# Stores of the twenty-product sums moved to GpSimd's queue, and the kept sums weighed one block later

## The chip, the cores and the metric

The kernel runs on one core of a Trainium2 chip. Its time is device microseconds (us) for one execution; several executions were timed, and the figure given is their median. A profile of one execution, taken by the hardware profiler, stands beside it.

The engines of a core run side by side and each works through its own list of instructions in order. TensorE (PE in the profile) multiplies matrices, and its weight loads (PEld) overlap its multiplications. VectorE (DVE) and ScalarE (ACT) do elementwise work and evict accumulators. GpSimd (POOL) does elementwise work too. SyncE (SP) does nothing here but issue transfers. A transfer is issued by an engine's list, so an engine that waits before it issues one transfer issues none of the later ones either.

## The reference, cut to what matters

An attention block gives a matrix x of 4352 rows and 128 columns. Then comes a mixture of eight experts, with all eight weighted by P, which is found from x by eight rounds of normalization:

```python
for e in range(E):                       # E = 8
    h = np.maximum(x @ w1[e], 0.0)       # w1[e]: 128 x 1024
    ye = h @ w2[e]                       # w2[e]: 1024 x 128
    out += P[:, e:e + 1] * ye
```

All of it is in 32-bit floats. P is positive, so the weight can be put on x before the first product instead of on ye after the second.

## The kernel before: the parts concerned

The rows of x are split into groups. The first groups use experts 0 and 1 and run while P is not yet known; their results stay unweighted in SBUF, in tiles called `kept`. Then come five groups of three tiles of 256 columns each (`t == 3` below), for the remaining experts, and a last group of two tiles. A pair of a group and an expert is an item. An item of a three-tile group has two blocks of eight steps.

The second product of such an item is done with twenty smaller products in place of twenty-four, and for it sixteen of the twenty need sums and differences of blocks of w2. In the first three-tile group GpSimd computes these sums for each expert, once, and the result (128 partitions x 2048 floats, 1 MB) is stored to memory. The later groups load them back.

```python
def sums_of_four(e, w2):
    ws = pools[0].tile([P, len(FORMS), FO // 4, H2], F32, tag="ws4", name="ws4")   # two buffers
    if e in stored_four:
        nc.sync.dma_start(out=ws, in_=stored_four[e])            # L230: later groups load
        return ws
    ...
    for ns, x, y, off in FOURS:                                  # ten instructions, L242
        tc.keep_in_program_order(nc.gpsimd.tensor_tensor(ws[:, c:c + len(ns)], blocks(x), blocks(y), ...))
        c += len(ns)
    stored_four[e] = dram.tile([P, len(FORMS), FO // 4, H2], F32, name=f"ws4{e}")
    nc.sync.dma_start(out=stored_four[e], in_=ws)                # L246: the store
    return ws
```

The weights of expert e are loaded by SyncE, w1 by L190 and w2 by L191. The weighted input of an item, `xe`, is made by a load of P's row spread over the partitions (L674, SyncE) and a product with x on GpSimd (L678). The `kept` tiles are weighed in the same way, from a buffer called `pb`:

```python
def load_w(e, ...):
    w1 = wpool.tile([P, F], F32, tag="w1", name="w1")                        # two buffers of each
    w2 = wpool.tile([P, FO, DM], F32, tag="w2", name="w2")
    nc.sync.dma_start(out=w1, in_=moe_w1[e])                                 # L190
    nc.sync.dma_start(out=w2, in_=moe_w2[e].rearrange(...))                  # L191

def weights_of(e, lo, n, tag):
    pb = pools[0].tile([P, 3 * NT3], F32, tag=tag, name=tag)[:, 0:n]         # two buffers
    tc.keep_in_program_order(nc.sync.dma_start(out=pb, in_=pT[e:e + 1, lo:lo + n].to_broadcast([P, n])))  # L674
    return pb

def weigh(out, x, pb):
    tc.keep_in_program_order(nc.gpsimd.tensor_tensor(out, x, pb, op=Alu.mult))                            # L678

def weigh_kept(g, i):
    lo, n, t, es, _ = groups[g]
    ys = [kept[e][:, lo:lo + n * t] for e in range(es[0])]
    if i < len(ys):
        weigh(ys[i], ys[i], weights_of(i, lo, n * t, "pb"))
        return
    for y in ys[1:]: ...                                                     # L702: the second is added to the first
```

At the first block of an item (q == 0) the next item is prepared:

```python
if q == 0:
    for i in (j, j + 1, ...):
        ... prepare_x(i)        # xe: L674, L678
        ... prepare_w(i)        # w1, w2, and sums_of_four
...
if q == 0:
    if weighted and 1 <= es.index(e) <= es[0] + 1:
        weigh_kept(g, es.index(e) - 1)
```

TensorE's part is two functions. The first product of a step is L914 (`a<-xe,w`), evicted by ScalarE (L918). The twenty products are L1099 (`s<-hx,ws`, `s<-hb,ws`, and with `w` where no sum is needed); they follow the first products of their block by eight steps, that is by one block.

Of the kernel before, what the change touches and what calls it, by code (L numbers as in the profile page):

```python
# [50 lines left out]
def kernel(  # L51
# [12 lines left out]
    nc = tc.nc  # L64
# [147 lines left out]
    stored, stored_four = {}, {}  # L212
# [13 lines left out]
    def sums_of_four(e, w2):  # L226

        ws = pools[0].tile([P, len(FORMS), FO // 4, H2], F32, tag="ws4", name="ws4")
        if e in stored_four:
            nc.sync.dma_start(out=ws, in_=stored_four[e])  # L230
            return ws

        def blocks(bs):
            b = w2[:, bs[0][1]::4, H2 * bs[0][0]:H2 * (bs[0][0] + 1)].unsqueeze(1)
            if len(bs) == 1:
                return b
            step = (bs[1][1] - bs[0][1]) * DM + (bs[1][0] - bs[0][0]) * H2
            return AP(tensor=b.tensor, offset=b.offset, ap=[b.ap[0], [step, 2], *b.ap[2:]])

        c = 0  # L240
        for ns, x, y, off in FOURS:
            tc.keep_in_program_order(nc.gpsimd.tensor_tensor(ws[:, c:c + len(ns)], blocks(x), blocks(y),  # L242
                                                             op=Alu.subtract if off else Alu.add))
            c += len(ns)
        stored_four[e] = dram.tile([P, len(FORMS), FO // 4, H2], F32, name=f"ws4{e}")
        nc.sync.dma_start(out=stored_four[e], in_=ws)  # L246
        return ws


# [399 lines left out]
    def direct_of(j):  # L649
        return items[j][0] in DIRECT  # L650
# [4 lines left out]
    def prepare_w(j):  # L655
        g, e = items[j]
        three = groups[g][2] == 3
        if j == 0:
            loaded_w[j] = first_w
        elif items[j - 1][1] == e or not groups[g][4]:  # L660
            before = [i for i in range(j) if items[i][1] == e and i in loaded_w]
            loaded_w[j] = loaded_w[before[-1]] if before else load_w(e, False)
            if three and tiles_of(j - 1) == 2:
                loaded_w[j] = *loaded_w[j][0:2], sums_of_four(e, loaded_w[j][1])
        else:
            loaded_w[j] = load_w(e, not three, again=groups[g][4])
            if three:
                if g == len(groups) - 2 and e in groups[-1][3]:
                    sums_of_two(e, loaded_w[j][1], True)
                loaded_w[j] = *loaded_w[j][0:2], sums_of_four(e, loaded_w[j][1])  # L670

    def weights_of(e, lo, n, tag):
        pb = pools[0].tile([P, 3 * NT3], F32, tag=tag, name=tag)[:, 0:n]
# [6 lines that stand above are left out]
    def prepare_x(j):  # L680
        g, e = items[j]
        lo, n, t, es, weighted = groups[g]
        x = xT[:, lo:lo + t * n]
        if not weighted:
            sources[j] = x
            return
        xe = weights_of(e, lo, t * n, "xe")
        for sl in (slice(0, 512), slice(512, 768)) if j == first_weighted else (slice(0, t * n),):
            weigh(xe[:, sl], x[:, sl], xe[:, sl])
        sources[j] = xe  # L690
# [3 lines left out]
# [7 lines that stand above are left out]
        for y in ys[1:]:  # L701
            tc.keep_in_program_order(nc.gpsimd.tensor_tensor(ys[0], ys[0], y, op=Alu.add))  # L702
        if t == 2:
            k1, k2 = ys[0][upper, 0:n], ys[0][upper, n:2 * n]
            tc.keep_in_program_order(nc.gpsimd.tensor_tensor(k1, k1, k2, op=Alu.subtract))
# [335 lines left out]
    def last_products():  # L1041

        k = len(blocks) - 2
        one, two_ = ([[(b, p) for p in ps] for ps in seven(b)] for b in (k, k + 1))
        f = last_rooms(len(groups) - 1)[4]
        return one + held[:2] + two_ + held[2:4] + [[(k + 1, (both, f, 2, 0, 0))]] + held[4:]

    def kept_to_sums(g):

        lo, n, *_ = groups[g]  # L1050
        k1, k2 = (kept[0][:, lo + t * n:lo + (t + 1) * n] for t in range(2))
        for i, s, x in ((1, 0, k1), (1, 1, k1), (2, 0, k2), (3, 1, k2)):
            into(g, ident[:, H2 * s:H2 * (s + 1)], x, i, s, 0)
# [52 lines left out]
    def second(k, p):  # L1106
        into(items[blocks[k][0]][0], *p)

    def steps():

        todo, sums_at, t = {}, {}, 0
        for k in range(len(blocks) + 5):
            if k == len(blocks) - 2:
                ctx.enter_context(tc.manual_schedule(engines={engines.DVE, engines.PE, engines.Activation}))
            if k == len(blocks):
                for i, ps in enumerate(last_products()):
                    todo.setdefault(t + i, []).extend(ps)
            if k < len(blocks):
                j, q = blocks[k]
                g, e = items[j]  # L1120
                lo, n, tiles, es, weighted = groups[g]
                if q == 0:
                    for i in (j, j + 1, j + 2 if 0 < j and j + 2 < first_weighted else j):
                        if i < len(items) and i not in sources and (pools or i < first_weighted):
                            prepare_x(i)
                        if i < len(items) and i not in loaded_w and (pools or i < first_weighted):
                            prepare_w(i)
                if j == 0 and q == 2:
                    prepare_w(2)
                if q == 1 and j + 1 < first_weighted and not direct_of(j + 1) and loaded_w[j + 1][2] is None:  # L1130
                    w1, w2, _ = loaded_w[j + 1]
                    w = w1, w2, sums_of_two(items[j + 1][1], w2)
                    loaded_w.update({i: w for i in loaded_w if items[i][1] == items[j + 1][1]})
                if q == 0:
                    if weighted and 1 <= es.index(e) <= es[0] + 1:
                        weigh_kept(g, es.index(e) - 1)
                if k == len(blocks) - HELD:
                    kept_to_sums(g)
                m, step, sums_ = (four if tiles == 3 else two)(k)
                products = twenty if tiles == 3 else eight if g in DIRECT else seven  # L1140
            for c in range(m if k < len(blocks) else 4):
                if k < len(blocks):
                    step(c)
                for do in sums_at.pop(t, ()):
                    do()
                while soon:
                    soon.pop(0)()
                for b, p in todo.pop(t, ()):
                    second(b, p)
                if k < len(blocks) and c == 0:  # L1150
                    for i in range(2, 10):
                        sums_at.setdefault(t + i, []).append(lambda i=i, f=sums_: f(i))
                    if k < len(blocks) - 2:
                        for i, ps in enumerate(products(k)):
                            todo.setdefault(t + LAG + i, []).extend((k, p) for p in ps)
                share = n / 480 * (16 / 15 if g in DIRECT else 1)
                if k >= len(blocks):
                    while later:
                        later.pop(0)()
                elif later and (tiles == 3 or c % 2 or share > 0.9):  # L1160
                    later.pop(0)()
                yield share
                t += 1
        while soon:
            soon.pop(0)()
        while later:
            later.pop(0)()

    work = steps()
    owed = [0.0]

# [97 lines left out]
```

## Time and profile before

| | before |
|---|---|
| time, median of 3 | 920.12 us (920.08 to 920.75) |
| span in the profile | 918.0 us |
| TensorE busy | 911.2 us (99%) |
| VectorE busy | 678.9 us (74%) |
| ScalarE busy | 421.6 us (46%) |
| GpSimd busy | 204.0 us (22%) |
| mean transfer rate | 140 GB/s |
| first three-tile group, seven items | about 184 to 318 us of the span |
| stores concerned (L246) | 7 of 1024 KB, issued from 191.6 to 307.5 us, 4.7 to 5.1 us to landing |

In the views, a line names the source line of the kernel, the engine, the operation, what it writes and from what (`ws<-w`), and how often. In a timeline the first two columns are the start and the length in us, and a bracket at the end says how long the engine sat idle before and what released it. SPq is SyncE's list, which only issues transfers; it is not counted as busy. "xe<-pT" is the load of a row of P.

### The profile page before, as it was taken

How to read it: one execution, taken by the hardware profiler on the slowest of the kernel's cores; microseconds unless marked ns; L12 is line 12 of the kernel's file. 1: busy time of each engine (PE TensorE's matmuls, PEld its weight loads, DVE VectorE, ACT ScalarE, POOL GpSimd, SP SyncE). 2: the span in 40 equal slices, each digit the busy share in tenths (PEclk: the TensorE clock that was granted, in tenths of full speed). 3: DMA queues.
4: the chain of work that ended last, by engine and by line, in shares of the span. 5: the costliest groups of instructions: out<-in, count | busy, mean ns of one | idle time of the engine just before them, and what ended most of it. 6: DMA issues, size and time to landing. Idle time of an engine off the chain costs nothing.

```text
span 918.0 us, 18893 instructions
## 1 busy us (share of the span) xinstructions
PE 911.2 (99%) x7442; PEld 637.4 (69%) x7442; DVE 678.9 (74%) x1173; ACT 421.6 (46%) x915; POOL 204.0 (22%) x212
## 2 busy tenths in 40 slices
PE   9999999999999999999999999999999999999997
PEld 6777544466666677777777777777777655556886
DVE  7678699888776798666975656956567976758665
ACT  3455555554444454444544444544445444445443
POOL 3121100175545421201210010110100243210220
PEclk9999999999999999999999999999999999999999
DMA  9994100213454535534364343454445456453640
GB/s 254 308 273 163 54 1 1 70 64 127 148 150 139 186 119 174 165 110 150 114 185 134 117 143 112 132 187 127 133 122 165 130 170 195 162 166 92 177 153 13
DMA packets 91305, 128.15 MB, mean 140 GB/s; under 512 B 25392, under 2 KB 69504, under 8 KB 86480
## 3 DMA queue, kind: packets, MB, share of 16 engines
q1 hardware_dynamic: 88384, 121.42, 42.7%
q0 software_dynamic: 1600, 5.36, 2.1%
q8 instruction: 58, 0.95, 0.4%
q10 hardware_dynamic: 1232, 0.16, 0.1%
q14 instruction: 31, 0.25, 0.1%
HBM read 107.88 MB, written 19.05 MB: 138 GB/s over the span
## 4 chain that ended last, share of the span: by engine, by line
PE 97%; DVE 2%; ACT 1%; issue 0%; POOL 0%; DVEq 0%; POOLq 0%
PE a L914 51%; PE s L1099 41%; PE a L347 1%; PE a L462 1%; PE a L114 1%; DVE hb L931 1%; PE a L314 0%; PE s L376 0%; PE a L426 0%; PE s L392 0%; DVE cs L602 0%; PE a L496 0%; PE a L392 0%; ACT hb L918 0%; DVE rs L596 0%
## 5 line engine op out<-in xcount | busy, mean ns | idle before, releaser
L914 PE MATMUL a<-xe,w 128*64 128x256 f32 (+1 forms) x2560 | 569.8, 470 | 0.0
L918 ACT ACTIVATE hb<-a 128x256 f32<-128x256 f32 (+4 forms) x408 | 195.0, 480 | 241.5 <-PE a L914 209.3
L914 PEld LDWEIGHTS a<-xe,w 128*64 128x64 f32 x2560 | 263.0, 137 | 50.8 <-issue 1.8
L918 ACT ACTIVATE hx<-a 128x256 f32<-128x256 f32 (+1 forms) x360 | 167.3, 465 | 213.5 <-PE a L914 191.6
L1099 PE MATMUL s<-hb,ws 128*64 128x256 f32 (+3 forms) x1312 | 256.1, 395 | 0.2 <-DVE hb L931 0.2
L1099 PE MATMUL s<-hx,ws 128*64 128x256 f32 x1280 | 233.9, 379 | 0.0
L978 DVE TENSOR_TENSOR hb<-hb 128x512 f32<-128x512 f32 (+1 forms) x204 | 133.5, 664 | 102.8 <-ACT hb L918 98.8
L978 DVE TENSOR_TENSOR hx<-hx 128x512 f32<-128x512 f32 (+1 forms) x204 | 149.8, 744 | 65.0 <-ACT hx L918 60.2
L1099 PEld LDWEIGHTS s<-hb,ws 128*64 128x64 f32 x1312 | 134.9, 137 | 87.8 <-issue 64.5
L678 POOL TENSOR_TENSOR xe<-xT,xe 128x768 f32<-128x768 f32 (+2 forms) x41 | 80.3, 1958 | 481.2 <-DMA xe<-pT 377.0
L1099 PEld LDWEIGHTS s<-hx,ws 128*64 128x64 f32 x1280 | 132.7, 137 | 71.6 <-issue 50.3
L914 PE MATMUL a<-xT,w 128*64 128x416 f32 (+3 forms) x512 | 119.7, 462 | 0.0
L1099 PE MATMUL s<-hb,w 128*64 128x256 f32 (+3 forms) x536 | 114.2, 408 | 0.0
L1099 PE MATMUL s<-hx,w 128*64 128x256 f32 x384 | 76.0, 379 | 0.0
L931 DVE TENSOR_TENSOR hb<-hb 128x416 f32<-128x416 f32 (+7 forms) x84 | 60.7, 723 | 18.0 <-ACT hb L918 14.0
L1099 PEld LDWEIGHTS s<-hb,w 128*64 128x64 f32 x536 | 54.1, 137 | 19.0 <-issue 6.5
L914 PEld LDWEIGHTS a<-xT,w 128*64 128x64 f32 x512 | 48.9, 137 | 25.5 <-issue 15.7
L242 POOL TENSOR_TENSOR ws<-w 128x256 f32<-128x256 f32 (+1 forms) x70 | 60.5, 899 | 8.1 <-DMA w<-in_moe_w_dram 5.2
L931 DVE TENSOR_TENSOR hx<-hx 128x256 f32<-128x256 f32 (+1 forms) x65 | 39.5, 612 | 24.0 <-ACT hx L918 22.8
L1099 PEld LDWEIGHTS s<-hx,w 128*64 128x64 f32 x384 | 40.8, 137 | 6.6
L978 DVE TENSOR_TENSOR pqg<-hb 128x512 f32<-128x512 f32 x68 | 40.5, 637 | 0.0
L978 DVE TENSOR_TENSOR pqg<-hx 128x512 f32<-128x512 f32 x68 | 35.0, 554 | 0.0
(181 smaller groups left out, 485.0 us busy)
## 6 DMA issues: line engine op xcount, KB each, us to landing
w<-in_moe_w_dram SPq DMA_DIRECT2D x82, 512.0 KB, 5.5
ws<-ws SPq DMA_DIRECT2D x34, 1024.0 KB, 5.0
xe<-pT SPq DMA_DIRECT2D x34, 384.0 KB, 4.1
ws<-ws SPq DMA_DIRECT2D x12, 512.0 KB, 3.6
ph<-qa SPq DMA_DIRECT2D x12, 288.0 KB, 4.7
rb<-qb SPq DMA_DIRECT2D x3, 1152.0 KB, 7.2
pb<-pT SPq DMA_DIRECT2D x6, 384.0 KB, 8.3
kx<-in_k_dram SPq DMA_DIRECT2D x4, 544.0 KB, 4.0
```

Of the source, the lines that this page charges most:

```text
L114: nc.tensor.matmul(warm[:, 0:P], ones, ones, start=True, stop=True)
L242: tc.keep_in_program_order(nc.gpsimd.tensor_tensor(ws[:, c:c + len(ns)], blocks(x), blocks(y), op=Alu.subtract if off else Alu.add))
L347: nc.tensor.matmul(pv[64 * s:64 * (s + 1), i], kp[0:n, H * t + h].rearrange("p i j -> p (i j)"), vx[0:n, slots[h], t, :], start=(t == 0 an ...
L462: nc.tensor.matmul(pn[64 * s:64 * (s + 1), t, 2 * i:2 * i + 2].rearrange("p h d -> p (h d)"), ph[:, i, s, 64 * t:64 * (t + 1)], kvs[b % 2] ...
L678: tc.keep_in_program_order(nc.gpsimd.tensor_tensor(out, x, pb, op=Alu.mult))
L914: nc.tensor.matmul(ph[sl], loaded_w[j][0][:, P * f + H2 * s:P * f + H2 * (s + 1)], sources[j][:, lo:hi], start=True, stop=True, tile_posit ...
L918: nc.scalar.activation(out=out, in_=ph, func=Act.Relu)
L931: nc.vector.tensor_tensor(out, a, b, op=Alu.subtract)
L978: nc.vector.tensor_tensor(out if not isinstance(out, tuple) else places(*out), places(*a), places(*b) if isinstance(b, tuple) else b, op=A ...
L1099: nc.tensor.matmul(sums[g][i][H2 * s:H2 * (s + 1), n * place:n * (place + 1)], w, x, start=c == 1, stop=c == per, tile_position=(0, H2 * s))
```

## The change

The store of the sums is issued by GpSimd, in its program order, directly behind the ten instructions that make them, and no longer by SyncE. So SyncE no longer stands in front of the store until GpSimd is done, and what is behind it in SyncE's list, the next item's `xe` and w1, can be issued earlier. The weighing of the kept sums, with its load and GpSimd's product, moves from the first block of an item to the second.

```diff
         stored_four[e] = dram.tile([P, len(FORMS), FO // 4, H2], F32, name=f"ws4{e}")
-        nc.sync.dma_start(out=stored_four[e], in_=ws)
+        tc.keep_in_program_order(nc.gpsimd.dma_start(out=stored_four[e], in_=ws))
         return ws
...
-                if q == 0:
-                    if weighted and 1 <= es.index(e) <= es[0] + 1:
-                        weigh_kept(g, es.index(e) - 1)
+                if q == 1 and weighted and 1 <= es.index(e) <= es[0] + 1:
+                    weigh_kept(g, es.index(e) - 1)
```

The order of instructions on TensorE, VectorE and ScalarE is the same in both kernels. GpSimd's list gains the seven stores and is otherwise in the same order. SyncE's list loses them; apart from that only one load differs in place: the second `pb` of the next group (rows from 512) stands before the `xe`, w1, sums and w2 of an item instead of behind them.

## The prediction

> **What bounds the kernel now.** I read the busy shares by slice and the chain of waits of the page first, then the waits of TensorE alone, then SyncE's own waits, and last the timelines around the seven stores.
>
> ```profile
> PE   9999999999999999999999999999999999999997
> ...
> PE 97%; DVE 2%; ACT 1%; issue 0%; POOL 0%; DVEq 0%; POOLq 0%
> ```
>
> TensorE is at nine tenths or more in every slice but the last, and 97% of the chain that sets the end is TensorE's. GpSimd and SyncE, the only engines whose lists change, have no visible share. Busy matmuls are modelled, so I looked for hidden pauses too. TensorE's waits in the whole span are these three:
>
> ```profile
> PE a L114 <- POOL own L116: 1.0, 1, 1.0
> PE a L392 <- ACT kvz L362: 0.6, 1, 0.6
> PE s L1099 <- DVE hb L931: 0.2, 1, 0.2
> ```
>
> None is near a store. The busy time by stretch says the same: 20.00 of 20.00 us in every stretch from 200 to 400 us. And the pace is even: SyncE's w2 load, which waits for TensorE, goes out at 232.62, 251.57, 270.53 and 289.48 us, an item every 18.95 us; in the next group, where no store is made, at 365.29, 384.25 and 403.20, again 18.95. A stage slowed by the stores would show a longer item than one without them. So at most a fraction of a microsecond can be removed.
>
> Then, what the change aims at, from SyncE's waits (us in total, times, longest):
>
> ```profile
> SPq L674 <- PE a L914: 175.9, 23, 8.6
> ...
> SPq L246 <- POOL ws L242: 111.4, 7, 17.0
> ```
>
> SyncE stands 111.4 us in front of the seven stores until GpSimd has made the sums, with later loads behind it. Its timeline around the last store:
>
> ```profile
> 289.48 0.92 SPq L191 DMA_DIRECT2D w<-in_moe_w_dram  x1
> 307.52 0.33 SPq L246 DMA_DIRECT2D ws<-ws  x1
> 307.93 0.38 SPq L674 DMA_DIRECT2D xe<-pT  x1
> 308.37 0.91 SPq L190 DMA_DIRECT2D w<-in_moe_w_dram  x1
> 309.38 0.96 SPq L230 DMA_DIRECT2D ws<-ws  x1
> 310.40 0.64 SPq L191 DMA_DIRECT2D w<-in_moe_w_dram  x1
> 317.48 0.32 SPq L674 DMA_DIRECT2D xe<-pT  x1
> ```
>
> Five transfers go out within 3 us, 4 MB with the store. The item that uses this `xe` and w1 begins at 317.48 (that is when the next `xe` is released by TensorE). GpSimd's and the weight loads' timelines there:
>
> ```profile
> 299.62 7.87 POOL L242 TENSOR_TENSOR ws<-w 128x256 f32<-128x256 f32 x10 [2.74 <-DMA w<-in_moe_w_dram]
> 314.93 1.82 POOL L678 TENSOR_TENSOR xe<-xT,xe 128x768 f32<-128x768 f32 x1 [7.44 <-DMA xe<-pT]
> ```
>
> ```profile
> 317.07 0.35 PEld L1099 LDWEIGHTS s<-hx,w 128*64 128x64 f32 x2
> 317.60 0.26 PEld L914 LDWEIGHTS a<-xe,w 128*64 128x64 f32 x4 [0.17 <-issue]
> ```
>
> The `xe` is ready at 314.93 + 1.82 = 316.75, 0.7 us early. The w1, issued at 308.37, took 9.1 us to land by the line's own view: 317.47. Its first weight load stands at 317.60, after 0.17 us of idle time; the matmuls behind it start at 317.63, 0.34 us after those before them at 317.29, where 0.21 is the pace. This is the one pause, about 0.13 us, that I can tie to the stores.
>
> **What the Trainium skill says.** "DMA: Bandwidth & Descriptors", section "Issuing engines are not separate DMA queues", says that transfers issued by SyncE, ScalarE and GpSimd run on the same 16 DMA engines, and that a second issuing engine saves only the sequencer's time, which is usually small. Here the traces show why it is not small: the sequencer is not busy but waits, in order, 17.0 us at most. The same page, section "Anatomy of one DMA — SWDGE (gpsimd) path", fits a GpSimd transfer as about 2.0 us plus the bytes at 436 GB/s. For 1,048,576 bytes that gives an estimate of 4.4 us; SyncE's stores took 4.7 to 5.1 us, so no great change is to be expected. "SBUF — State Buffer", section "SBUF: two separate sides", warns that GpSimd cannot write descriptors while certain VectorE instructions hold their shared port. The trace has GpSimd's other transfers: issuing one took 0.54 to 0.64 us on average by line (L433, L437, L486, L488), with VectorE busy beside it. So the warning does not show as a large cost.
>
> **The change part by part.**
> 1. SyncE loses seven issues of 0.33 us and 111.4 us of standing still. Neither is on the chain. What counts is how late its followers come. The needed times: an item starts every 18.95 us, at 241.7, 260.6, 279.6, 298.5 and 317.5; its `xe` and w1 are needed then, its sums one block, 9.5 us, later (the first L1099 weights of the last item are loaded at 308.03, so this fits). Before, `xe` was ready at 240.2, 258.6, 277.5, 296.9 and 316.75: margins of 1.5, 2.0, 2.1, 1.6 and 0.7 us. The last sums were ready at 299.62 + 7.87 = 307.49: a margin of 0.5 us. Everything was just in time.
> 2. Afterwards `xe` and w1 go out when TensorE frees their buffers, at the item's start: for the last one 298.5 instead of 307.9. `xe` lands about 4.1 us later (median of its row), w1 about 5.5 us later (median of its row): 304. w2, issued at 289.48, lands with less beside it: 289.48 + 5.5 = 295.0 instead of 299.6. The ten sums run from 295.0 to 303.8 (8.8 us as in the items before), the store's issue to 304.4, the weighing of `xe` to 306.2. Needed at 317.5: a margin of 11 us instead of 0.7. For the sums 308.0 - 303.8 = 4.2 us instead of 0.5. Gained on the chain: the 0.13 us pause.
> 3. GpSimd gains seven issues of about 0.6 us, 4 us on an engine busy for 9.3 to 11.7 of each 20 us there. Cost on the chain: 0.
> 4. The move by a block: GpSimd's order stays, so the product with `kept` (1.8 to 2.3 us) stands between the same neighbours. On SyncE one `pb` issue (0.57 us) comes ahead of an `xe` that TensorE frees at 355.42. The twelve output stores before it end at 354.2; adding 0.57 gives 354.75, still earlier. And that `xe` was ready at 359.75 + 1.92 = 361.7 for an item that begins at 374.4. Cost: 0. In the last group the lists are the same; its final `kept` is ready at 877.7 and used at 882.4 us.
>
> The sum is -0.13 us, rounded by the spread of the times before (0.67 us) to "no change that matters": 919.97, written as 920.0.
>
> **The rivals.** (a) The stores held TensorE up unseen, and freeing SyncE brings several microseconds. For it: 111.4 us of standing, margins of 0.5 to 2 us. Against it: the same 18.95 us per item with and without stores. It would make some 910 to 917. (b) GpSimd becomes the late one: if a store's issue took as long as a VectorE stretch of work, say 5 us, the sums of the next item would still have 4 us of margin and `xe` 11, so seven such issues cost nothing; only at 10 us each would TensorE wait, some 5 us each, 7 x 5 = 35 us, 955 in all. The 0.6 us issues before speak against it. (c) The store, now free to collide with other loads, delays w2 of the next item. By the times above it runs from 304 to 309 for the last item, while w2 of the item after needs TensorE at 308.5; in the middle items the store ends before w2 is issued (265 to 270, w2 at 270.5). A delay of 1 to 2 us would be taken from a margin of 4. No time. (d) The pause at 317.5 disappears but the two halves of the array run on in another phase: before it the weight loads are 13.2 us per 20, after it 15.6, at the same pace per item. A tenth of a microsecond either way at later changes of shape.
>
> **Range and chances.** The three times before spread by 0.67 us, and the effects named are 0.1 to 0.2 us. So eight in ten lie within about 0.6 us of 920.0: 919.4 to 920.6. Two per cent is 18 us, which neither rival (a) nor anything seen can bring: 0.01 faster. Rival (b) at its worst reaches it: 0.01 slower. Within 2%: 0.98.
>
> **What would show it right or wrong.** Right: SyncE's wait for the sums is gone from its waits, with L674 and L190 issued at item starts; TensorE's pace stays 18.95 us; no 0.17 us idle time at the weight load near 317.5; `xe` and the sums ready 4 to 11 us ahead; GpSimd has seven issues of about 0.6 us. Wrong: new waits of TensorE for GpSimd or for a transfer, items longer than 18.95 us between 200 and 320 us, GpSimd issues of many microseconds, or a time outside the range with a pace that did change, which would mean that "busy" hid a slower TensorE.

## The result and the profile after

| | before | after |
|---|---|---|
| time, median | 920.13 us (919.5 to 920.75) | 923.76 us (922.61 to 924.81, and one of 1063.66) |
| span in the profile | 918.0 us | 921.1 us |
| TensorE busy | 911.2 us | 911.6 us |
| VectorE busy | 678.9 us | 689.0 us |
| GpSimd busy | 204.0 us | 206.5 us |

One of the six executions of after ran at a granted clock of 0.851 and took 1063.66 us; the median of the other five is 923.67 us, and the ratios in this text are of executions at full clock alone. The ratio of after to before is 1.0036, with a 95% interval of 1.0023 to 1.0050. The kernel became slower by 2 to 5 us: less than 2%, but more than its spread, and outside the range that was predicted.

Two of TensorE's waits are new. One, 0.5 us for `kT` (L302), is at 7.5 us of the span, before anything that the change touches: the first load of `kx` landed later in this execution. It comes and goes between the kernels below (0 to 1.3 us) and is no effect of the change. The other is one (us in total, times, longest):

```profile
PE s L1099 <- DVE hx L978: 2.2, 2, 2.0
```

Twenty-product matmuls waited 2.0 us for VectorE, and 0.2 us once more at 205.5 us, not for GpSimd or for a transfer. TensorE's timeline of after at the long wait:

```profile
198.95 0.59 PE L914 MATMUL a<-xe,w 128*64 128x256 f32 x2
201.54 0.65 PE L1099 MATMUL s<-hx,ws 128*64 128x256 f32 x4 [2.00 <-DVE hx L978]
```

What held VectorE stands in its own timeline of after:

```profile
193.17 7.46 DVE L741 TENSOR_TENSOR z<-x,z 128x384 f32<-128x384 f32 x1 [1.77 <-ACT x L750]
200.55 0.94 DVE L978 TENSOR_TENSOR hx<-hx 128x512 f32<-128x512 f32 x1
```

The same addition before:

```profile
192.62 0.56 DVE L741 TENSOR_TENSOR z<-x,z 128x384 f32<-128x384 f32 x1 [1.77 <-ACT x L750]
```

One addition of 384 columns took 7.46 us instead of 0.56. It is counted as busy, so the page shows no wait of VectorE, only 10 us more of busy time, 6.9 of them in this addition. GpSimd's timeline of after says what ran beside it:

```profile
192.43 0.60 POOL L246 DMA_DIRECT2D ws<-ws  x1 [0.30 <-POOL ws L242]
193.05 1.83 POOL L678 TENSOR_TENSOR xe<-xT,xe 128x768 f32<-128x768 f32 x1
194.84 6.10 POOL L242 TENSOR_TENSOR ws<-w 128x256 f32<-128x256 f32 x10
201.23 0.61 POOL L246 DMA_DIRECT2D ws<-ws  x1 [0.30 <-POOL ws L242]
```

The addition lasts from 193.17 to 200.63, that is, from just behind the first store's issue to near the end of eleven GpSimd products without a pause. (GpSimd's spans in a profile are rough; by them the addition ended 0.3 us before the last of the eleven, so some ten of them went ahead of it.) The products were fast for it: ten sums in 6.10 us, against 7.87 to 9.13 us before. In the kernel before, the second item's product came only at 197.6 us, because its `xe` waited behind the store in SyncE's list; the addition at 192.6 had no GpSimd product beside it.

What the change was for did happen. SyncE's wait for the sums is gone from its list of waits, and the last item of the group had its `xe` at 305.97 + 1.82 = 307.8 for a start at 320.8 us: 13 us ahead instead of 0.7.

### The profile page after: what moved, and what is told of

Same layout as the page of the kernel before. It is cut to its first block, busy times and chain, and to the rows that moved or that the text cites. A ratio compares the mean times of both kernels' runs of the same rounds, so it can differ in the third digit from the quotient of the medians.

```text
span 921.1 us, 18899 instructions
## 1 busy us (share of the span) xinstructions
PE 911.6 (99%) x7442; PEld 533.8 (58%) x7442; DVE 689.0 (75%) x1173; ACT 421.7 (46%) x915; POOL 206.5 (22%) x219
## 4 chain that ended last, share of the span: by engine, by line
PE 95%; DVE 3%; ACT 1%; DMA 1%; issue 0%; SPq 0%; DVEq 0%; ACTq 0%
PE a L914 49%; PE s L1099 42%; PE a L347 1%; DVE z L741 1%; PE a L462 1%; DMA kx<-in_k_dram 1%; DVE hb L931 1%; PE a L314 0%; PE s L376 0%; PE a L426 0%; DVE hx L978 0%; PE s L392 0%; DVE cs L602 0%; PE a L496 0%; PE a L392 0%
## 5 line engine op out<-in xcount | busy, mean ns | idle before, releaser
L914 PE MATMUL a<-xe,w 128*64 128x256 f32 (+1 forms) x2560 | 516.2, 470 | 0.0
L914 PEld LDWEIGHTS a<-xe,w 128*64 128x64 f32 x2560 | 200.1, 137 | 86.6 <-issue 1.6
L1099 PE MATMUL s<-hb,ws 128*64 128x256 f32 (+3 forms) x1312 | 228.7, 395 | 0.2 <-DVE hb L931 0.2
L978 DVE TENSOR_TENSOR hb<-hb 128x512 f32<-128x512 f32 (+1 forms) x204 | 132.2, 658 | 102.2 <-ACT hb L918 98.5
L1099 PE MATMUL s<-hx,ws 128*64 128x256 f32 x1280 | 205.4, 379 | 2.2 <-DVE hx L978 2.2
L978 DVE TENSOR_TENSOR hx<-hx 128x512 f32<-128x512 f32 (+1 forms) x204 | 156.3, 777 | 57.5 <-ACT hx L918 52.4
L1099 PEld LDWEIGHTS s<-hb,ws 128*64 128x64 f32 x1312 | 104.9, 137 | 116.7 <-issue 86.6
L1099 PEld LDWEIGHTS s<-hx,ws 128*64 128x64 f32 x1280 | 102.4, 137 | 103.2 <-issue 74.2
L1099 PE MATMUL s<-hb,w 128*64 128x256 f32 (+3 forms) x536 | 106.9, 408 | 0.0
L1099 PE MATMUL s<-hx,w 128*64 128x256 f32 x384 | 67.8, 379 | 0.0
L1099 PEld LDWEIGHTS s<-hb,w 128*64 128x64 f32 x536 | 46.8, 137 | 24.0 <-issue 6.5
L978 DVE TENSOR_TENSOR pqg<-hb 128x512 f32<-128x512 f32 x68 | 41.3, 649 | 0.0
L1099 PEld LDWEIGHTS s<-hx,w 128*64 128x64 f32 x384 | 33.2, 137 | 11.5
L978 DVE TENSOR_TENSOR pqg<-hx 128x512 f32<-128x512 f32 x68 | 36.4, 575 | 0.0
```

Source lines behind the costliest of these rows:

```text
L914: nc.tensor.matmul(ph[sl], loaded_w[j][0][:, P * f + H2 * s:P * f + H2 * (s + 1)], sources[j][:, lo:hi], start=True, stop=True, tile_posit ...
L978: nc.vector.tensor_tensor(out if not isinstance(out, tuple) else places(*out), places(*a), places(*b) if isinstance(b, tuple) else b, op=A ...
L1099: nc.tensor.matmul(sums[g][i][H2 * s:H2 * (s + 1), n * place:n * (place + 1)], w, x, start=c == 1, stop=c == per, tile_position=(0, H2 * s))
```

## The experiments

Three theories stood at first. **A:** GpSimd's products for the second item start 4.6 us earlier, and so collide with a busy stretch of VectorE; any kernel with so early a product stalls. **B:** it is the later weighing of the kept sums that costs the time. **C:** it is the issuing of a transfer by GpSimd that lets VectorE be held. Each kernel was timed against the kernel before on the same chip, in three rounds.

**The store alone.** The weighing of the kept sums stays at the first block:

```diff
-        nc.sync.dma_start(out=stored_four[e], in_=ws)
+        tc.keep_in_program_order(nc.gpsimd.dma_start(out=stored_four[e], in_=ws))
```

> Only the store moves to GpSimd's queue; the kept sums are weighed at the first block as before. Theory A (the stall is one VectorE addition, z<-x,z near 193 us, held off by GpSimd's back-to-back products for 7.5 us because the product for the second item now starts at 193 instead of 197.6 us): the same stall, 2 to 3 us of TensorE's time, 922.5 to 924.5 us. Rival B (the later weighing of the kept sums, which lines up two GpSimd products at 230 us, costs the time): 920.

Measured: 923.03 us, ratio 1.0034 (1.0023 to 1.0046). The addition took 7.75 us, and TensorE waited 2.3 us for hx L978. The store carries the loss; A and C both expect this, B does not.

**The weighing alone.** The stores stay with SyncE; the weighing moves to the second block:

```diff
-                if q == 0:
-                    if weighted and 1 <= es.index(e) <= es[0] + 1:
+                if q == 1 and weighted and 1 <= es.index(e) <= es[0] + 1:
```

> Only the weighing moves by a block; the stores stay with SyncE. Theory A: no stall near 199 us, 919.5 to 920.7 us. Rival B: 922.5 to 924.5.

Measured: 920.57 us, ratio 1.0004 (0.9996 to 1.0013). The addition took 0.56 us. B falls.

**The store by SyncE, but late.** Against after:

```diff
-        tc.keep_in_program_order(nc.gpsimd.dma_start(out=stored_four[e], in_=ws))
+        owed_stores.append((stored_four[e], ws))
...
         xe = weights_of(e, lo, t * n, "xe")
+        pay_stores()          # nc.sync.dma_start for each one owed
```

> The changed kernel, but each store is issued by SyncE, behind the load of the next xe. GpSimd issues no transfer, and its product for the second item can still follow the first sums at once, at about 192 us. Theory A, from the early product: z<-x,z is held off again, for 1.8 us at least and perhaps to the end of the sums (about 200), 920.5 to 924. Rival C (it is GpSimd's writing of the transfer's descriptors that holds VectorE): z<-x,z takes 0.6 us as before and the time is 920.

Measured: 919.97 us, ratio 1.0000 (0.9991 to 1.0008). GpSimd's product came even earlier than in after, and VectorE was not held for long. The timelines of this kernel, VectorE first:

```profile
192.66 1.15 DVE L749 TENSOR_TENSOR z<-x,z 128x384 f32<-128x384 f32 x1 [1.77 <-ACT x L758]
193.73 1.22 DVE L986 TENSOR_TENSOR hx<-hx 128x512 f32<-128x512 f32 x1
```

```profile
191.57 1.82 POOL L685 TENSOR_TENSOR xe<-xT,xe 128x768 f32<-128x768 f32 x1
193.34 10.92 POOL L249 TENSOR_TENSOR ws<-w 128x256 f32<-128x256 f32 x10
```

(Line numbers are shifted by the edit: L749 is the addition, L249 the sums.) Here the two engines take turns: the two VectorE instructions take 1.15 and 1.22 us where they took 0.56 and 0.69 in the kernel before, and the ten sums take 10.92 us instead of 6.10. Theory A falls: the same early products, no stall. Theory C is left, though it had expected 0.6 us for the addition and not 1.15.

**The first store by SyncE, six by GpSimd.** Against after:

```diff
-        tc.keep_in_program_order(nc.gpsimd.dma_start(out=stored_four[e], in_=ws))
+        if e == 1:
+            nc.sync.dma_start(out=stored_four[e], in_=ws)
+        else:
+            tc.keep_in_program_order(nc.gpsimd.dma_start(out=stored_four[e], in_=ws))
```

> The changed kernel, but the first of the seven stores stays with SyncE, so that the second item's xe comes as late as before (product at 197.6). Theory A: no stall near 199 us, z<-x,z 0.6 us, 919.5 to 920.6. Rival C: six stores remain on GpSimd, each of which can hold VectorE; 922 to 924.

Measured: 921.05 us, ratio 1.0009 (1.0002 to 1.0015), between the two expectations. The long hold at 193 us is gone. A short one is left behind the second store, where a single product follows: hb<-hb at 210.0 took 2.82 us, and TensorE waited 0.64 us for it at 212.9. So a store's cost depends on how many products stand behind it, and on VectorE's slack there.

From this came theory **D**: a transfer issued by GpSimd opens a time in which a VectorE addition that comes up is held through all GpSimd products that follow without a pause. It says nothing of the transfer's size. Its rivals are that size counts (**E**) and that only the phase counts in which the addition meets the product (**F**).

**A small transfer in the store's place.** Against the kernel with SyncE's late stores:

```diff
         owed_stores.append((stored_four[e], ws))
+        if e == 1:
+            tiny = dram.tile([P, 16], F32, name="tiny")
+            tc.keep_in_program_order(nc.gpsimd.dma_start(out=tiny, in_=ws[:, 0, 0, 0:16]))
```

> The stores stay with SyncE behind the next xe's load (that kernel took 919.97 us and held nothing); added is one small transfer, 8 KB, issued by GpSimd between the first sums and the second item's product, where the changed kernel has its first 1 MB store. Theory D (issuing any transfer on GpSimd opens a time in which a VectorE addition that comes up behind it is held through all GpSimd products that follow without a pause): z<-x,z is held 7 to 8 us, TensorE waits 2 to 3 us, 922 to 923.5 us. Rival E (it is the 1 MB store's size, its many descriptors or its data): z<-x,z takes 0.6 to 1.2 us, 919.5 to 920.6.

Measured: 922.68 us, ratio 1.0025 (1.0016 to 1.0034). VectorE and GpSimd in this kernel:

```profile
192.63 6.86 DVE L752 TENSOR_TENSOR z<-x,z 128x384 f32<-128x384 f32 x1 [2.02 <-ACT x L761]
```

```profile
191.29 0.60 POOL L256 DMA_DIRECT2D tiny<-ws  x1
191.92 1.82 POOL L688 TENSOR_TENSOR xe<-xT,xe 128x768 f32<-128x768 f32 x1
193.69 6.11 POOL L249 TENSOR_TENSOR ws<-w 128x256 f32<-128x256 f32 x10
```

8 KB do what 1 MB did: held 6.86 us, slightly less than the 7 to 8 expected since it came up 0.7 us behind the product's start. TensorE waited 1.6 us. E falls.

**A memset in its place.**

```diff
+        if e == 1:
+            idle = pools[0].tile([P, 640], F32, name="idle", bufs=1)
+            tc.keep_in_program_order(nc.gpsimd.memset(idle, 0.0))
```

> As the one with the small transfer, but a memset of 640 columns (some 0.6 us of GpSimd) in the transfer's place, so that the product for the second item starts at the same 193 us with no transfer. Theory D: no long hold, z<-x,z at most 2.3 us, 919.5 to 920.6. Rival F (it is the phase in which VectorE's addition meets GpSimd's product, 0.1 us behind its start): held 7 to 8 us again, 922 to 923.5.

Measured: 920.39 us, ratio 1.0000 (0.9991 to 1.0008). The memset took 0.63 us, the product started at 192.48, and the addition, 0.5 us behind that, took 1.74 us; after it the engines took turns. As long an occupation of GpSimd without a transfer does nothing. VectorE's and GpSimd's lines:

```profile
192.98 1.74 DVE L752 TENSOR_TENSOR z<-x,z 128x384 f32<-128x384 f32 x1 [1.77 <-ACT x L761]
```

```profile
191.89 0.63 POOL L256 MEMSET idle<- 128x640 f32 x1
```

The addition came 0.5 us behind the product's start and not 0.1, so this run alone does not settle F. Taken together the runs do. The held instructions came up between 0.15 us before (the store alone) and 0.7 us behind (the small transfer) the start of the `xe` product; with no transfer ahead, an addition 0.5 us behind it passed here, and an hx<-hx 0.03 us behind a product with sums following (the weighing alone, at 198.4) took 2.34 us, no more than that one product explains. The same phases come with and without a hold, so F falls.

**The first store behind the second item's sums.** All seven stores on GpSimd's queue:

```diff
-        tc.keep_in_program_order(nc.gpsimd.dma_start(out=stored_four[e], in_=ws))
+        owed_stores.append((stored_four[e], ws))
+        while e > 1 and owed_stores:
+            to, x = owed_stores.pop(0)
+            tc.keep_in_program_order(nc.gpsimd.dma_start(out=to, in_=x))
```

> The changed kernel with all seven stores on GpSimd's queue, but the first is issued behind the second item's sums, together with the second store, where no run of ten products follows. Theory D: no hold of 7 us, none of TensorE's waits near 199 us, 919.5 to 920.8. Rival (any store on GpSimd's queue costs about 0.4 us each): 922 to 923.5.

Measured: 920.48 us, ratio 1.0000 (0.9991 to 1.0009). The addition took 1.27 us, and the loss is gone with every store still on GpSimd. It is not a price of each store; it is what stands behind the first one.

**The addition from PSUM.** Against after, the held addition takes its first operand from the accumulator instead of its copy in SBUF:

```diff
-            add_now(z, p, z)
+            add_now(z, s, z)
```

> The changed kernel, but the addition that was held reads its first operand from PSUM, so it has one SBUF input. If the hold concerns VectorE instructions with two SBUF inputs alone, this addition takes 0.5 to 0.8 us at 193 us, and the next one behind it with two SBUF inputs (hx<-hx) is held instead, some 6 to 7 us; TensorE's wait stays 1.5 to 3 us and the time 921.5 to 923.8. If any VectorE instruction is held, the addition itself takes 7 us again.

Measured: 922.86 us, ratio 1.0026 (1.0017 to 1.0034). VectorE:

```profile
192.81 0.56 DVE L741 TENSOR_TENSOR z<-s,z 128x384 f32<-128x384 f32 x1 [1.75 <-ACT x L750]
193.31 7.13 DVE L978 TENSOR_TENSOR hx<-hx 128x512 f32<-128x512 f32 x1
```

With one operand in PSUM the addition passes in 0.56 us beside GpSimd's product, and the next, with both operands in SBUF, is held 7.13 us in its stead.

**A pause behind the transfer.** As with the small transfer, but its landing place is in SBUF, and GpSimd waits for it:

```diff
+            tiny = pools[0].tile([P, 16], F32, name="tiny", bufs=1)
+            tc.keep_in_program_order(nc.gpsimd.dma_start(out=tiny, in_=ws[:, 0, 0, 0:16]))
+            tc.keep_in_program_order(nc.gpsimd.memset(tiny, 0.0))
```

> As the one with the small transfer, but GpSimd waits for its landing (a memset of the landing place in SBUF) before it takes the second item's product. Theory D says that the hold lasts only while GpSimd goes on without a pause: after a pause of some 2 us no long hold, no VectorE instruction above 2.4 us near 193 to 206 us, 919.5 to 920.8 us. If a transfer changes GpSimd's behaviour for longer, a hold of some 7 us again and 922 to 923.5.

Measured: 920.41 us, ratio 1.0003 (0.9994 to 1.0011). The pause was 4.4 us, so the product came at 197.36, where w<-w,r met it 0.003 us before its start, was held 2.24 us (the one product), and then the engines took turns. A pause ends the effect. It is not the landing by itself that ends it: the small transfer of the earlier run landed 4.4 us after its issue, and the hold there went on until 8.2 us after it. The pause also moved the products; the memset run above shows that an early product alone is harmless.

**The small transfer at another place.** Ahead of the ten sums of expert 5:

```diff
+        if e == 5:
+            tiny = dram.tile([P, 16], F32, name="tiny")
+            tc.keep_in_program_order(nc.gpsimd.dma_start(out=tiny, in_=w2[:, 0, 0:16]))
```

> Stores with SyncE as in the kernel of 919.97 us, and one small transfer of GpSimd directly ahead of the ten sums of another expert (e = 5), at about 256 us, where no addition of the kept parts is about. Theory D: the first VectorE instruction with two SBUF inputs that comes up then (hb<-hb, 0.5 us without the transfer) is held 5 to 7 us to near the end of the ten sums; TensorE waits if that is more than the slack there, 920 to 923 us. If the hold belongs to the place at 193 us and its instructions alone, every instruction there stays below 1.3 us and the time is 920.

Measured: 920.24 us, ratio 1.0000 (0.9991 to 1.0009). GpSimd and VectorE in this kernel, two VectorE instructions in the one line:

```profile
256.48 0.60 POOL L249 DMA_DIRECT2D tiny<-w  x1 [8.41 <-PE a L925]
257.10 5.99 POOL L252 TENSOR_TENSOR ws<-w 128x256 f32<-128x256 f32 x10
```

```profile
256.88 6.75 DVE L989 TENSOR_TENSOR hb<-hb 128x256 f32<-128x256 f32 x2 [0.87 <-ACT hb L929]
```

The first of the two, 0.50 us long in the kernel without the small transfer, took 5.89 us. It is the same hold, on other instructions at another time. TensorE did not wait for VectorE here, where VectorE is not adding kept parts and has the slack. The hold is the cause, and the loss comes only where it falls on a VectorE that is late already.

The changed kernel has the hold a second time. Behind its third store two products follow without a pause, from 230.05 to 233.65 us, and VectorE shows:

```profile
229.72 4.22 DVE L998 TENSOR_TENSOR hb<-pqg,hb 128x256 f32<-128x256 f32 x1
```

This instruction takes 0.43 us at 267.8. All five kernels with this store on GpSimd's queue have one instruction of 3.99 to 4.23 us there; with the stores late on SyncE the same two products follow each other too, but two instructions shared the wait, 1.93 and 2.31 us. TensorE waited in none of them, so this hold costs nothing.

## Why the prediction was wrong, point by point

- **What bounds the kernel: right.** TensorE is the bound. What was lost is behind its new waits: 2.2 us of them in the view, 2.8 us by what TensorE releases. (SyncE's w2 load went out at 216.99 instead of 213.67 us: 3.3 us later, less 0.55 us that the execution was behind before any store.) From there the pace is again 18.95 us an item. The two spans differ by 3.1 us: this loss and the 0.55 us of `kx`, less some 0.2 us that fall away late in the span.
- **What the skill says: misapplied.** The passage of "SBUF — State Buffer", section "SBUF: two separate sides", was read in one direction alone: VectorE holding up GpSimd's descriptors. The same section says that the pair of ports goes to one engine for a whole instruction, against VectorE instructions with two SBUF inputs if the GpSimd instruction reads SBUF. The traces agree for single products (VectorE instructions beside the 1.8 us product of `xe` took 1.6 to 1.7 us more: 2.18, 2.34, 2.24) and for the PSUM operand (0.56 us). It does not say what happens from one GpSimd instruction to the next: with no transfer ahead the two took turns; behind a transfer, some ten products in a row went first.
- **Steps 1 and 2: right in what they said.** `xe` came 11 to 13 us ahead and the sums 6, the pause at 317.5 us was gone. The gain of 0.13 us from it does not show: TensorE's releases are 3.3 us late at 217 us and still at 329. (The five transfers near 307.5 us carry 3.4 MB, not 4.) The steps asked only whether GpSimd's work comes in time, not what it does to others when it comes earlier.
- **Step 3 is the one that failed:** "Cost on the chain: 0". The issue itself took 0.59 to 0.61 us, as predicted. What it costs is not GpSimd's time but VectorE's: behind the store's issue a run of GpSimd's products held one addition 6.9 us longer, which cost about 2.8 us on the chain. With the first store behind that run, both were gone (1.27 us for the addition, 920.48 us in all).
- **Step 4: right.** The moved weighing alone measured no difference that can be seen.
- **The rivals.** Rival (b) had the right engine at work but the wrong one late. The phase of (d) did change, and at the same pace: between 222 and 320 us the weight loads are busy 10.8 to 11.0 of each 20 us, against 13.0 to 13.2 in the kernel before. None of the four named VectorE as the one held.

The page before had shown it already. Its timelines at 46 us, GpSimd and then VectorE:

```profile
46.17 0.59 POOL L486 DMA_DIRECT2D xd<-xt  x1 [4.51 <-DVE xt L481]
46.78 0.75 POOL L204 TENSOR_TENSOR ws<-ws,w 128x256 f32<-128x256 f32 x1
47.47 0.73 POOL L205 TENSOR_TENSOR ws<-w 128x256 f32<-128x256 f32 x1
48.16 0.73 POOL L206 TENSOR_TENSOR ws<-w,ws 128x256 f32<-128x256 f32 x1
```

```profile
45.97 3.73 DVE L931 TENSOR_TENSOR hb<-hb 128x576 f32<-128x576 f32 x3
```

A transfer, three products behind it, and three VectorE subtractions that took 3.73 us; the second of them alone took 2.45. That is the same picture, in a place where it cost TensorE nothing. The prediction looked at how long GpSimd's issues took there, and not at VectorE beside them.

What stays open: why GpSimd, behind a transfer, does not give way between products. The runs show that it needs a transfer, that 8 KB suffice, and that a pause ends it; they do not show the means. Nor do they show how short a pause suffices, or which instructions are caught that begin while the transfer is being issued: hb<-pqg,hb began 0.29 us into the issue both at 229.7 and at 267.8 us, and was held 4.22 us the first time and passed in 0.43 the second.

No version beat the kernel before: the margins gained on SyncE's side are worth nothing while nothing waits for them. The late stores by SyncE (919.97 us) give the margins without the loss.

## What to carry to other kernels

When an engine that is off the critical path is freed to work earlier, ask which engines share something with it, and look at what they do in the stretch of the trace into which it moves. Do not put a transfer on GpSimd's queue directly ahead of a run of its elementwise work while VectorE adds tiles in SBUF; put it behind the run, or on SyncE behind what must not wait. And a busy VectorE is not a working one: compare the time of single instructions with the same ones elsewhere.

## What was not expected of the hardware

- Behind a transfer issued by GpSimd, of 8 KB as of 1 MB, a VectorE instruction with both operands in SBUF took 5.9 to 7.7 us, to near the end of ten or eleven GpSimd products, and 4.0 to 4.2 us beside two longer ones; with no transfer ahead the same two engines took turns, and most VectorE instructions beside the sums took about 0.5 us more.
- GpSimd is fast while it does not give way: ten sums in 6.0 to 6.2 us during a hold, 7.9 to 10.9 us otherwise.
- The 1 MB store issued by GpSimd landed in 4.2 to 5.8 us in after, SyncE's in 4.7 to 5.1 us in before; where GpSimd issued two of them together, the slowest took 11.5 us.
